# Attention and feed-forward kernel on one core: the third chunk's scores from float32 keys on 64 rows of each head

## The chip, the cores and the metric

The kernel runs on one core of one Trainium2 chip. The metric is the device time of one launch in microseconds. The kernel before was run three times: 664.55, 667.24 and 668.45 us, so its median is 667.24 us.

## The reference

A sliding-window attention with sinks, followed by a two-layer feed-forward network. Four batches, eight heads, 768 positions, 64 features per head; each query sees the first 4 positions of its batch and the last 128 positions up to itself.

```python
scores = scale * np.matmul(q, k.transpose(0, 1, 3, 2))
keep = is_sink | in_window            # pos < n_sink, or 0 <= rel < window
scores = np.where(keep, scores, -1000000000.0)
a = np.exp(scores - max); a = a / (sum + 1e-09)
x = (a @ v) as [3072, 512]            # heads side by side
h = x @ w_in                          # 512 -> 2048
g = np.where(h > 0.0, h, np.exp(np.minimum(h, 0.0)) - 1.0)
out = g @ w_out                       # 2048 -> 512
```

## The kernel before, in words

The 3072 tokens are 24 tiles of 128, cut into nine chunks of 2, 2, 2, 3, 3, 3, 3, 3 and 3 tiles. Counted from 0, the third chunk is chunk 2; it holds the last two tiles of batch 0. For each chunk there is an attention part and a feed-forward part. The attention part goes through four pairs of heads; for each pair it loads the keys and queries, makes the scores of every tile (a query tile against one or two key tiles of 132 columns, 128 keys and 4 sinks), takes the row minimum and adds the mask on VectorE (L579), the exponential on ScalarE (L581), scales and splits the probabilities into two float16 parts (L593 and L594), transposes them by a DMA (L612, `pt<-pq`), and multiplies them with the split values (L623, L628) into `po`, from which `x` is made (L636, L637). The feed-forward part makes 16 slices `h` (L664), the nonlinearity (L672 to L678, of which L678 on GpSimd makes the low part `gl`), and adds `acc` (L685).

The weights come as float64 words. During the first 150 us every one of 32 pieces is loaded (L407, `raw`) and decoded: L276 and L277 on VectorE or L271 and L272 on GpSimd, L280 on ScalarE, L282 on VectorE, then split by L429 on ScalarE and L430 on GpSimd. The first two chunks' feed-forward is done in two halves, interleaved, so that the second half of the weights is needed later.

Scores are made in two ways, chosen by the chunk's number. With `c >= DUP` and `c >= WHOLE` each head has its keys and queries twice, on rows 0 to 63 and on rows 64 to 127 (the host lays them out so). ScalarE rounds all of it to fp32r (L496), GpSimd makes the low part of the keys (L500) and, on rows 64 to 127, of the queries (L502), and TensorE makes two fp32r matmuls per head and tile on 128 rows (L553, L554). With `c < WHOLE` the two heads of a pair lie side by side on 64 rows each, and TensorE reads them as float32 from where the DMA put them (L560), one matmul per head and tile, which the trace shows as two records each:

```python
if c < WHOLE:                                                   # L486
    ld = add("SP", 0.4, lambda: nc.sync.dma_start(st[:, :kw], kq[:, o : o + kw]), ...)
    return st, None, ld, ld, users
th = add("ACT", act_us(kw), lambda: nc.scalar.activation(hi, raw, AF.Copy), deps=[ld])   # L496
```

The loads go through two buffers, `kqs0` and `kqs1`, in turn. A head's load with `c >= DUP` may overwrite its buffer once L496 and L502 have read it (L506). With `c < WHOLE` there is one load for the pair, and the buffer is free once the scores of all the chunk's tiles of that pair are made on TensorE (L574, L575). The fp32r keys go through three buffers, `kq0` to `kq2`, which are free once the scores read them (L507).

The order on every engine is written out by a planner (class `Plan`). TensorE's order is sorted by a position: slice `f` of a chunk's feed-forward has a fixed place, the scores and the value products are spread between them. The other engines and the DMA queue of SyncE (SP) are ordered by a model with costs and due times; each instruction is then chained to the one before it on its engine, so each engine and the SP queue run strictly in that order, and an instruction that waits holds up all that stand behind it.

## Time and profile before

| | us |
|---|---|
| median of three runs | 667.24 |
| lowest, highest | 664.55, 668.45 |
| span of the profiled execution | 665.4 |
| TensorE busy in the span | 610.5 |
| VectorE busy | 460.1 |
| ScalarE busy | 436.2 |
| GpSimd busy | 390.2 |

The page gives the profiled execution by its span, from the first to the last instruction; it has no other time of that execution. The median of the runs is 1.84 us above this span. The profile names the engines PE (TensorE), DVE (VectorE), ACT (ScalarE), POOL (GpSimd) and SP (the DMA queue of SyncE). In the timelines a row begins with the start and the length in us; at its end, in square brackets, stands how long the engine had been idle before it, and what released it. Rows of equal instructions that follow each other are one row, with their number behind an x.

### The profile page before, as it was taken

Reading aid. Unit: us, or ns where it says so; the run is one execution under the profiler, and the core shown is the slowest. Engines: PE = TensorE matmul, PEld = TensorE weight load, DVE = VectorE, ACT = ScalarE, POOL = GpSimd, SP = SyncE. Lnnn points to the kernel's source line nnn. Section 1 sums busy time; section 2 is a strip of 40 time slices with the busy share of each in tenths; the row PEclk is TensorE's granted clock in tenths of the full one; section 3 lists DMA queues with packets and bytes.
Section 4 is the critical chain, followed back from the end, with each engine's and each line's share of the span. In section 5 each row is a group of like instructions: output and inputs, shape, how many; then the busy total and the mean of one; then the engine's idle time right before and its main releaser. Section 6 shows DMA issues by size and latency. Waiting matters only on the chain.

```text
span 665.4 us, 13447 instructions
## 1 busy us (share of the span) xinstructions
PE 610.5 (92%) x4449; PEld 369.7 (56%) x4449; DVE 460.1 (69%) x1235; ACT 436.2 (66%) x1212; POOL 390.2 (59%) x641
## 2 busy tenths in 40 slices
PE   3477589899999999999999999999999999999995
PEld 2244356556666655555555556565555565555552
DVE  6888799997778765657677767767777776624222
ACT  4888677787778877666667776666667766523221
POOL 3599987887557766555556665554556674322221
PEclk9999689899999999999999999999999999999998
DMA  7889975746645474445444565546456723311001
GB/s 251 201 286 250 224 241 183 251 128 177 148 123 151 120 171 122 104 106 170 115 142 119 149 149 154 98 105 188 107 157 128 208 72 94 70 51 49 1 0 54
DMA packets 130110, 93.41 MB, mean 140 GB/s; under 512 B 104432, under 2 KB 109552, under 8 KB 130032
## 3 DMA queue, kind: packets, MB, share of 16 engines
q1 hardware_dynamic: 130032, 92.47, 52.2%
q8 instruction: 37, 0.61, 0.4%
q14 instruction: 41, 0.34, 0.2%
HBM read 59.94 MB, written 7.34 MB: 101 GB/s over the span
## 4 chain that ended last, share of the span: by engine, by line
PE 68%; DVE 7%; POOL 3%; DMA 3%; ACT 2%; issue 1%; POOLq 0%; ACTq 0%
PE acc L685 30%; PE h L664 30%; PE po L623 4%; PE s L553 2%; PE s L554 2%; DMA pt<-pq 2%; DVE g L674 1%; DVE wu L277 1%; DVE pq L594 1%; POOL kq L502 1%; POOL kq L500 1%; DVE wv L282 1%; POOL gl L678 1%; DVE g L675 1%; DVE wu L276 1%
## 5 line engine op out<-in xcount | busy, mean ns | idle before, releaser
L664 PE MATMUL h<-x,w 128*128 128x384 f16 (+1 forms) x1728 | 276.9, 311 | 3.3 <-DVE g L675 2.4
L664 PEld LDWEIGHTS <-w 128*128 128x128 f16 x1728 | 165.1, 98 | 96.3 <-issue 5.5
L678 POOL TENSOR_TENSOR gl<-g,gh 128x384 f16<-128x384 f32 (+1 forms) x144 | 126.7, 880 | 153.9 <-ACT gh L677 142.0
L685 PE MATMUL acc<-w,gh 128*128 128x512 f16 x768 | 195.3, 384 | 0.0
L674 DVE TENSOR_SCALAR g<-g 128x384 f32<-128x384 f32 (+1 forms) x144 | 65.6, 456 | 118.1 <-ACT g L672 118.0
L594 DVE SCALAR_TENSOR_TENSOR pq<-e,st,pq 128x256 f16<-128x256 f32 (+1 forms) x192 | 112.6, 618 | 24.6 <-ACT pq L593 24.0
L672 ACT ACTIVATE g<-h 128x384 f32<-128x384 f32 (+1 forms) x144 | 65.0, 452 | 82.1 <-PE h L664 68.9
L677 ACT ACTIVATE gh<-g 128x384 f16<-128x384 f32 (+1 forms) x144 | 69.3, 482 | 73.2 <-DVE g L675 73.1
L685 PE MATMUL acc<-w,gl 128*128 128x512 f16 x384 | 110.2, 382 | 2.8 <-POOL gl L678 2.7
L685 PEld LDWEIGHTS <-gh 128*128 128x128 f16 x768 | 71.1, 98 | 70.3 <-issue 1.8
L581 ACT ACTIVATE e<-e,st 128x264 f32<-128x264 f32 (+1 forms) x192 | 93.3, 486 | 13.1 <-DVE st L579 11.4
L593 ACT ACTIVATE pq<-e,st 128x256 f16<-128x256 f32 (+1 forms) x192 | 83.8, 479 | 9.3 <-DVE st L586 3.8
L579 DVE CUSTOM_DVE_ANT_0 e<-s,m 128x264 f32<-128x264 f32 (+1 forms) x192 | 72.5, 402 | 18.9 <-PE s L554 15.9
L500 POOL TENSOR_TENSOR kq<-kqs,kq 128x396 fp32r<-128x396 f32 (+1 forms) x56 | 67.7, 1208 | 14.4 <-ACT kq L496 9.7
L675 DVE SCALAR_TENSOR_TENSOR g<-g,h 128x384 f32<-128x384 f32 (+1 forms) x144 | 72.4, 503 | 1.8
L685 PEld LDWEIGHTS <-gl 128*128 128x128 f16 x384 | 37.5, 99 | 50.5 <-POOL gl L678 5.5
L553 PE MATMUL s<-kq 128*128 128x264 f32 x160 | 55.8, 368 | 2.8 <-POOL kq L502 2.4
L502 POOL TENSOR_TENSOR kq<-kqs,kq 64x384 fp32r<-64x384 f32 (+1 forms) x56 | 55.8, 996 | 4.4
L496 ACT ACTIVATE kq<-kqs 128x780 fp32r<-128x780 f32 (+2 forms) x56 | 48.3, 877 | 14.6 <-PE s L554 12.9
L623 PE MATMUL po<-pt,vh 128*64 128x128 f16 x704 | 42.3, 231 | 16.8 <-DMA pt<-pq 11.1
L585 POOL TENSOR_SCALAR st<-st 128x2 f32<-128x2 f32 x96 | 20.7, 216 | 59.1 <-ACT e L581 48.7
L623 PEld LDWEIGHTS <-vh 128*64 128x64 f16 x704 | 31.0, 115 | 29.2 <-issue 21.0
(80 smaller groups left out, 665.3 us busy)
## 6 DMA issues: line engine op xcount, KB each, us to landing
raw<-in_wt_dram SPq DMA_DIRECT2D x32, 512.0 KB, 5.5
kqs<-in_kq_dram SPq DMA_DIRECT2D x24, 456.0 KB, 3.3
kqs<-in_kq_dram SPq DMA_DIRECT2D x24, 390.0 KB, 3.2
out_dram<-wv SPq DMA_DIRECT2D x24, 256.0 KB, 2.3
vs<-in_vx_dram SPq DMA_DIRECT2D x20, 256.0 KB, 2.9
vm<-in_vx_dram SPq DMA_DIRECT2D x6, 768.0 KB, 4.7
kqs<-in_kq_dram SPq DMA_DIRECT2D x12, 326.0 KB, 3.7
vs<-in_vx_dram SPq DMA_DIRECT2D x12, 320.0 KB, 3.1
```

Of the source, the lines that this page charges most:

```text
L500: nc.gpsimd.tensor_tensor(buf[:, KQ_MAX : KQ_MAX + n] if c >= DUP else buf[:, kw : 2 * kw], raw[:, :n], hi[:, :n].bitcast(F32), ALU.subtract)
L579: red = add("DVE", 0.13 + 0.00145 * wd, lambda ee=ee, me=me, sp=sps[e], m=m, wd=wd: nc.vector.tensor_tensor_reduce(ee, sp[:, :wd], m[:, :w ...
L581: ex = add("ACT", 0.48 + 0.00085 * wd, lambda ee=ee, me=me, rs=rs[:, e : e + 1]: nc.scalar.activation(ee, ee, AF.Exp, bias=me, scale=-1.0, ...
L593: a = add("ACT", act_us(nb * P, True), lambda src=src, hi=hi, re=re: nc.scalar.activation(hi, src, AF.Copy, scale=re), deps=[rr])
L594: b = add("DVE", dve_us(nb * P) + 0.1, lambda src=src, hi=hi, lo=lo, re=re: nc.vector.scalar_tensor_tensor(lo, src, re, hi, ALU.mult, ALU. ...
L623: nc.tensor.matmul(po[e * D : (e + 1) * D, oc], vv[:, vo : vo + D], pt[:, (2 * e + part) * nb + i, :], start=new, stop=last)
L664: nc.tensor.matmul(hp[:, :n], win[:, part, d, :], xx[:, :n], start=k == 0, stop=k == 3 * ND - 1)
L674: b = add("DVE", 0.1 + 0.0008 * n, lambda gf=gf: nc.vector.tensor_scalar(gf, gf, -1.0, G_SCALE, ALU.add, ALU.mult), deps=[a])
L675: b = add("DVE", dve_us(n), lambda gf=gf, hp=hp: nc.vector.scalar_tensor_tensor(gf, gf, 0.0, hp[:, :n], ALU.min, ALU.max), deps=[b])
L677: th = add("ACT", act_us(n), lambda gf=gf, gh=gh: nc.scalar.activation(gh[:, :n], gf, AF.Copy), deps=[b])
L678: tl = add("POOL", pool_us(n), lambda gl=gl, gf=gf, gh=gh: nc.gpsimd.tensor_tensor(gl[:, :n], gf, gh[:, :n], ALU.subtract), deps=[th])
L685: nc.tensor.matmul(acc[i], gg[:, i * P : (i + 1) * P], wout[:, part, :], start=f == f0 and k == 0, stop=f == f1 - 1 and k == 2)
```

## The change

The scores of chunk 2 are made in the way of chunks 0 and 1. Both bounds, `WHOLE` and `DUP`, go from 2 to 3, and the layout that the host writes follows `DUP`.

```diff
 LAG = 2
-WHOLE = 2
-DUP = 2
+WHOLE = 3
+DUP = 3
 ON_POOL = range(0, 16, 2)
```

For chunk 2 the instructions of L496, L500 and L502 (eight of each) are gone, eight key loads of 128x652 become four, and 16 pairs of L553 and L554 become 16 matmuls of L560. The planner orders all engines anew.

On TensorE the places stay and only the scores change. This is the difference at the first scores of chunk 2; `s0` and `s1` are the two banks of the scores, `w9` and `w14` weight pieces.

```order
 L685 MATMUL acc1_170<-w9_141,gl1_115 128x512
-L553 MATMUL s0_166<-kq0_83 128x264
-L554 MATMUL s0_166<-kq0_83 128x264
-L553 MATMUL s1_167<-kq1_84 128x264
-L554 MATMUL s1_167<-kq1_84 128x264
+L560 MATMUL s0_166<-kqs0_70 128x264
+L560 MATMUL s1_167<-kqs0_70 128x264
 L664 LDWEIGHTS w14_146
 L664 MATMUL h1_165<-x_117,w14_146 128x256
```

Four fp32r matmuls have become two float32 matmuls, between the same neighbours.

On POOL, in the stretch just ahead of chunk 2's first scores, this stood before (`gl` is the low part of the nonlinearity, `vh0` the values' sink rows, `w` a weight piece, `wu` decoded words, `st` the softmax sums):

```order
L678 TENSOR_TENSOR gl0_114<-g1_110,gh0_111 128x256
L430 TENSOR_TENSOR w12_144<-wv0_120,w12_144 128x512
L271 TENSOR_SCALAR wu0_124<-raw2_128 128x512
L272 TENSOR_SCALAR wu0_124<-raw2_128 128x512
L529 COPY vh0_86<-vl0_88 8x128
L585 TENSOR_SCALAR st2_96<-st2_96 128x2
L678 TENSOR_TENSOR gl1_115<-g0_109,gh1_112 128x256
L500 TENSOR_TENSOR kq0_83<-kqs0_70,kq0_83 128x396
L502 TENSOR_TENSOR kq0_83<-kqs0_70,kq0_83 64x256
L500 TENSOR_TENSOR kq1_84<-kqs1_71,kq1_84 128x396
L502 TENSOR_TENSOR kq1_84<-kqs1_71,kq1_84 64x256
L585 TENSOR_SCALAR st3_97<-st3_97 128x2
```

And this stands there now:

```order
L678 TENSOR_TENSOR gl0_114<-g1_110,gh0_111 128x256
L600 TENSOR_TENSOR st0_94<-e0_91,st0_94 128x8
L603 CAST pq0_100<-st0_94 128x2x8
L604 TENSOR_TENSOR pq0_100<-st0_94,pq0_100 128x8
L272 TENSOR_SCALAR wu0_124<-raw0_126 128x512
L600 TENSOR_TENSOR st1_95<-e1_92,st1_95 128x8
L603 CAST pq1_101<-st1_95 128x2x8
L604 TENSOR_TENSOR pq1_101<-st1_95,pq1_101 128x8
L529 COPY vh0_86<-vl0_88 8x128
L430 TENSOR_TENSOR w9_141<-wv1_121,w9_141 128x512
L430 TENSOR_TENSOR w12_144<-wv0_120,w12_144 128x512
L678 TENSOR_TENSOR gl1_115<-g0_109,gh1_112 128x256
```

`gl0` has moved ahead of two groups of sink rows, of L272 and of `w9`; `vh0` has moved ahead of `w9`, of `w12` and of a pair of L271 and L272; the four key instructions between `gl1` and `st3` are gone.

On the SP queue, around the loads of chunk 3's first heads (128x780; `kqs0` for the even heads, `kqs1` for the odd ones), this stood before. `pt2` to `pt5` belong to the fifth to eighth of chunk 2's eight steps (a step is one pair of heads at one tile), `vs` is a load of values, `wv3` a reload of a saved partial sum:

```order
L520 DMA vs0_72<-in_vx_dram 128x512
L495 DMA kqs1_71<-in_kq_dram 128x780
L612 DMA_TRANSPOSE pt2_105<-pq2_102 128x9x128
L612 DMA_TRANSPOSE pt3_106<-pq0_100 128x9x128
L705 DMA wv3_123<-out_0_dram 128x512
L520 DMA vs1_73<-in_vx_dram 128x512
L495 DMA kqs0_70<-in_kq_dram 128x780
```

And this stands there now, where the first load into `kqs1` comes:

```order
L495 DMA kqs0_70<-in_kq_dram 128x780
L520 DMA vs0_72<-in_vx_dram 128x512
L612 DMA_TRANSPOSE pt4_107<-pq1_101 128x9x128
L495 DMA kqs1_71<-in_kq_dram 128x780
L612 DMA_TRANSPOSE pt5_108<-pq2_102 128x9x128
L495 DMA kqs1_71<-in_kq_dram 128x780
L612 DMA_TRANSPOSE pt0_103<-pq0_100 128x4x128
```

The load of chunk 3's second head, the first into `kqs1`, stood ahead of `pt2` and stands now between `pt4` and `pt5`; it waits there for TensorE, because the scores of chunk 2's last pair of heads read `kqs1` themselves.

## Rows read from the trace of the kernel before

**Rows 1.** The page, its first line and part 1: busy time of each engine in us, share of the span, instructions.

```profile
span 665.4 us, 13447 instructions
...
PE 610.5 (92%) x4449; PEld 369.7 (56%) x4449; DVE 460.1 (69%) x1235; ACT 436.2 (66%) x1212; POOL 390.2 (59%) x641
```

**Rows 2.** Busy time of each engine in stretches of 20 us (us from the start, length, busy us of each engine with the number of instructions), then the granted TensorE clock, the busy share of the DMA engines and GB/s.

```profile
60.00:80.00 20.00, 11.35 (x89) 6.78 (x83) 15.63 (x33) 13.93 (x38) 18.46 (x27) 0.74 0.95 264
80.00:100.00 20.00, 16.24 (x124) 10.88 (x125) 18.55 (x39) 15.60 (x41) 17.25 (x25) 0.91 0.86 217
100.00:120.00 20.00, 17.11 (x137) 11.64 (x135) 19.32 (x38) 14.28 (x40) 14.96 (x22) 0.98 0.61 182
120.00:140.00 20.00, 18.21 (x135) 11.77 (x133) 20.00 (x44) 16.86 (x45) 16.41 (x22) 0.93 0.61 203
140.00:160.00 20.00, 18.70 (x148) 12.72 (x146) 15.98 (x40) 14.20 (x45) 16.86 (x29) 1.00 0.71 182
```

**Rows 3.** TensorE's timeline from 60 to 157 us: the rows with the longest waits.

```profile
62.82 0.30 PE L623 MATMUL po<-pt,vh 128*64 128x128 f16 x4 [2.70 <-DMA pt<-pq]
...
67.83 0.87 PE L685 MATMUL acc<-w,gl 128*128 128x512 f16 x2 [2.15 <-POOL gl L678]
...
72.50 0.32 PE L628 MATMUL po<-pt,vh 128*64 128x128 f16 x2 [3.02 <-POOL vh L529]
...
80.04 1.38 PE L664 MATMUL h<-x,w 128*128 128x256 f16 x11 [0.83 <-POOL w L430]
84.67 0.30 PE L623 MATMUL po<-pt,vh 128*64 128x128 f16 x4 [3.25 <-DMA pt<-pq]
...
118.52 2.08 PE L664 MATMUL h<-x,w 128*128 128x256 f16 x12 [1.43 <-DVE g L675]
```

**Rows 4.** POOL's timeline from 67 to 78 us, with the first four key instructions of chunk 2.

```profile
67.10 0.68 POOL L678 TENSOR_TENSOR gl<-g,gh 128x256 f16<-128x256 f32 x1
...
72.16 0.28 POOL L529 COPY vh<-vl 8x128 f16<-8x128 f16 x1
...
73.43 1.50 POOL L500 TENSOR_TENSOR kq<-kqs,kq 128x396 fp32r<-128x396 f32 x1
75.01 0.79 POOL L502 TENSOR_TENSOR kq<-kqs,kq 64x256 fp32r<-64x256 f32 x1
75.88 1.08 POOL L500 TENSOR_TENSOR kq<-kqs,kq 128x396 fp32r<-128x396 f32 x1
77.03 0.72 POOL L502 TENSOR_TENSOR kq<-kqs,kq 64x256 fp32r<-64x256 f32 x1
```

**Rows 5.** The timelines of VectorE and of POOL from 93 to 98 us: one VectorE operation without and with a key instruction beside it, and the key instructions.

```profile
93.33 0.45 DVE L277 TENSOR_SCALAR wu<-raw 128x512 uint16<-128x512 uint16 x1
...
96.86 1.29 DVE L277 TENSOR_SCALAR wu<-raw 128x512 uint16<-128x512 uint16 x1
...
96.75 1.08 POOL L500 TENSOR_TENSOR kq<-kqs,kq 128x396 fp32r<-128x396 f32 x1
97.91 0.80 POOL L502 TENSOR_TENSOR kq<-kqs,kq 64x256 fp32r<-64x256 f32 x1
```

**Rows 6.** TensorE's timeline: a pair of heads by float32 matmuls in chunk 1, back to back and behind a wait, and a pair by fp32r matmuls in chunk 2, each with the row that follows it.

```profile
50.29 0.72 PE L560 MATMUL s<-kqs 64*128 64x264 f32 x4
50.93 1.48 PE L664 MATMUL h<-x,w 128*128 128x256 f16 x12
...
54.59 1.06 PE L560 MATMUL s<-kqs 64*128 64x264 f32 x4 [0.88 <-DVE st L579]
55.59 0.30 PE L623 MATMUL po<-pt,vh 128*64 128x128 f16 x4
...
102.18 0.48 PE L553 MATMUL s<-kq 128*128 128x264 f32 x1
...
102.86 1.48 PE L664 MATMUL h<-x,w 128*128 128x256 f16 x12
```

**Rows 7.** The start of chunk 3: TensorE's last scores of chunk 2 and what follows, then ScalarE's and POOL's work on the keys of chunk 3's second head, then TensorE's scores of that head.

```profile
156.51 0.48 PE L553 MATMUL s<-kq 128*128 128x264 f32 x1
...
157.19 1.49 PE L664 MATMUL h<-x,w 128*128 128x256 f16 x12
...
157.27 0.84 ACT L496 ACTIVATE kq<-kqs 128x780 fp32r<-128x780 f32 x1
...
158.19 1.02 POOL L500 TENSOR_TENSOR kq<-kqs,kq 128x396 fp32r<-128x396 f32 x1
159.29 1.14 POOL L502 TENSOR_TENSOR kq<-kqs,kq 64x384 fp32r<-64x384 f32 x1
...
160.48 0.33 PE L553 MATMUL s<-kq 128*128 128x132 f32 x1 [0.35 <-POOL kq L502]
```

**Rows 8.** Key loads: two loads of chunk 1 on the SP queue in one row (the first stands at its start), the scores that waited for the first of them, and, from the view of L495, the time from issue to landing of its 56 loads.

```profile
38.85 5.31 SPq L489 DMA_DIRECT2D kqs<-in_kq_dram  x2
...
44.73 0.90 PE L560 MATMUL s<-kqs 64*128 64x264 f32 x4 [0.93 <-DMA kqs<-in_kq_dram]
...
DMA to landing us min/median/max: 3.0/3.3/6.3
```

**Rows 9.** TensorE's timeline from 165 to 240 us: two waits that remain.

```profile
183.04 0.30 PE L623 MATMUL po<-pt,vh 128*64 128x128 f16 x4 [0.97 <-DMA pt<-pq]
...
216.45 0.39 PE L553 MATMUL s<-kq 128*128 128x264 f32 x1 [1.22 <-POOL kq L502]
```

## The prediction

> **What bounds the kernel now.** I read the page's first part, then the busy times by stretches of 20 us, then TensorE's timeline where these show holes, and last the timelines of the engines that ended its waits. TensorE is busy 610.5 of 665.4 us [rows 1], so little but its own idle time and its clock can be gained. From 60 to 160 us it is busy for 81.61 of 100 us (the sum of the five stretches, 11.35 to 18.70), at a granted clock down to 0.74 [rows 2]. In these 100 us POOL is busy for 83.94 and VectorE for 89.48; VectorE has no pause at all from 120 to 140 us, and the DMA engines are at 0.95 from 60 to 80 us [rows 2]. So this stage, where the weights are decoded beside the attention of chunks 1 to 3, is bounded by POOL first and by VectorE later, and TensorE waits for them. Its long waits are of that kind: 2.15 us for `gl`, 3.02 for `vh`, 0.83 for a weight piece (all three made by POOL), 2.70 and 3.25 for transposed probabilities, 1.43 for VectorE [rows 3]. From 160 us on TensorE is nearly always at work, and only an added wait there would count.
>
> **The change, part by part.** All is summed against the span of the profiled execution, 665.4 us; the median of the runs is 667.24, so 1.84 us more, and I carry the difference over to the median.
>
> *TensorE's scores.* A pair by fp32r takes from 102.18 to 102.86, 0.68 us; a pair by float32 takes from 50.29 to 50.93, 0.64 us, back to back behind other matmuls, and 1.00 us (54.59 to 55.59) behind a wait [rows 6]. Chunk 2 has eight such pairs and most stand between busy neighbours: 8 x -0.04 = -0.3 us. Bounds: -0.3 to 8 x 0.32 = +2.6.
>
> *A rule that speaks against the change* is in the Trainium skill, "FP8 and Floating Point Precision", section "TensorE Precision Notes": a true float32 matmul goes through the array in four passes. As an estimate by that page, two heads of four passes of 264 columns at 2.4 GHz are 0.88 us a pair, and the term would be 8 x 0.20 = +1.6 us in place of -0.3. The row with 0.64 us is below that, so I keep the row.
>
> *Less work on POOL, ScalarE and the DMA queue.* Eight L500 and eight L502 go; the four that the rows show take 1.50, 0.79, 1.08 and 0.72, together 4.09 us from 73.43 on [rows 4], so the eight heads are some 15 to 16 us of POOL (1.88 for the head at 96.75 [rows 5]), of the 83.94 that it works in this stage. Eight ScalarE copies and four of eight loads go as well.
>
> What of this reaches TensorE: the wait of 0.83 for a weight piece and that of 3.25 for transposes come behind the four key instructions, whose 4.09 us stand ahead of `st3` and what follows it; both go, -4.1. The waits for `gl` (2.15) and `vh` (3.02) come ahead of them, but the planner has moved both instructions forward on POOL, `gl0` past an L272, the piece `w9` and six short ones, `vh0` past `w9`, `w12` and a pair of L271 and L272; what it moved back is still owed, so I count half of 5.17, -2.6. The clock of 0.74 and 0.91 in the first two stretches stands for some 10.4 and 3.6 us at 1.2 in place of 2.4 GHz (twice the missing share of 20 us); less the 3.02 us of waiting among them, half of the rest, 5.5 us, is what this costs, and with less idle time I count a quarter of it, -1.4. Sum: -8.1 by the end of chunk 2.
>
> Is VectorE able to follow? From 80 to 140 us it is busy for 57.87 of 60 us [rows 2], so TensorE can keep a lead only if VectorE gets through earlier as well. The rows say that it does: L277 takes 0.45 us alone and 1.29 beside a key instruction [rows 5], 0.84 us given back per L500. If a head costs it one such delay and a fourth more for its L502, eight heads give back 8 x 1.05 = 8.4 us. That covers the lead, but barely. Bounds of the whole gain: below nothing, +2.7 us, if the planner's new order of the early loads, with the DMA engines at 0.95, repeats the wait of 2.70 at one more place; at most the four waits (9.25) and all the lost clock (5.5), -14.8. I take -8.1.
>
> *A new wait at the start of chunk 3.* Before, the keys of chunk 3's second head were loaded long ahead; what ended last was the fp32r buffer, free after chunk 2's last scores: ScalarE copies at 157.27, POOL makes the low parts from 158.19 to 160.43, TensorE goes on at 160.48, 0.35 us late [rows 7]. Now `kqs1` is read by chunk 2's last scores themselves, so the load can only be issued after these, and the same copy and low parts come after the load. What is added to the path is the load: 3.3 us (3.0 to 6.3) and some 0.15 for the queue, +3.45. Between them TensorE has the same work as before, one `h`, one `acc` and the first head's scores, so nothing hides it. Behind the waiting load on SP stand `pt5`, the load of the fourth head and `pt0`; `pt5` needs the same scores and its values are due much later, so they cost nothing more. A load that waited in the same manner in chunk 1 was issued at 38.85 and its scores came at 44.73 [rows 8], 5.9 us, with the DMA engines busier. Bounds: 3.1 to 6.5.
>
> TensorE would then idle for 0.35 + 3.45 = 3.8 us. After the waits of 3.02 and 3.25 it ran at 1.2 GHz for a while (clock 0.74 and 0.91 in these stretches [rows 2, 3]); I add 1.5 us for that, between 0 and 2. Once TensorE is late by this, a wait such as the 0.97 us at 183.04 shrinks, while the 1.22 at 216.45 hangs on TensorE's own scores and stays [rows 9]: -0.5.
>
> Sum: -0.3 - 8.1 + 3.45 + 1.5 - 0.5 = -3.95 us. From 667.24 that is 663.3.
>
> **The rivals.**
>
> *The gain is larger.* All four waits on POOL go (-9.25) with half of the lost clock (-2.7), and the new wait costs its smallest value, 3.1, without a fall of the clock: -0.3 - 11.95 + 3.1 = -9.15 us, 658.1. For it: POOL is the busiest engine from 60 to 80 us. Against it: VectorE's 57.87 of 60 us afterwards, which can give back 8.4 at best by the rows.
>
> *Given back.* VectorE stays the bound up to 140 us, and its delays beside key instructions turn into delays beside L430 and `gl`, which move up into the free places. Then the lead at chunk 2's end is what VectorE saves, perhaps half of 8.4, 4.2 us, and the new wait takes it: -0.3 - 4.2 + 4.45 = 0, 667.2. A price of float32 pairs of 1.00 us, as behind a wait, ends here too: -3.95 + 2.9 = -1.05, 666.2. The four passes of the Trainium skill's page would put it at -3.95 + 1.9 = -2.05, 665.2, by that estimate.
>
> *Slower.* The load at chunk 3's start costs what the one at 38.85 cost, 5.9 us in place of 3.3, since `pt4`, itself late if TensorE runs ahead of the engines that make it, stands before it on SP: 5.9 + 0.15 + 2 for the clock = +8.05, and the lead is only 3, since the waits for `gl` and `vh` reappear as waits for the weight pieces that were moved back: 667.24 - 0.3 + 8.05 - 3 = 672.0. It decides as soon as the new wait with its clock is over 3.3 us more than the lead. For it: the load has nothing to hide behind. Against it: from 140 to 160 us the DMA engines are at 0.71 only.
>
> That the change doesn't do what it says can be left out: the order shows all eight pairs as float32.
>
> **How the numbers follow.** Half a per cent, 3.3 us, is about what a measurement of this kernel can tell from no change. Chances: the sum above, taken as faster by over 3.3 us, 0.34; the larger gain 0.13; given back, within 3.3 us on either side, 0.34; slower 0.19. That makes faster 0.47, same 0.34, slower 0.19. (Of the 0.34, 0.05 stand for dearer float32 pairs, by the row of 1.00 us.) The rule of the Trainium skill's page would come out in that same part. The predicted time is that of the sum, 663.3, whose own range is 660 to 664. The range for 8 in 10 reaches from 656, below the larger gain's 658.1 but short of the bound of -14.8, to 670.5, short of the slower case's 672.0.
>
> **What would show it right or wrong.** Right: chunk 2's last scores come some 8 us earlier than 156.51; the waits for `vh` and for the weight piece between 60 and 90 us are gone; VectorE's L277 in this stage has fewer long instances; TensorE waits some 3.8 us at the first scores of chunk 3's second head, with the load of these keys, ScalarE's copy and POOL's low part before it; from there to the end the distance is that of before plus what the clock loses. Wrong: chunk 2's last scores come less than 5 us earlier (then the lead was mis-sized), the wait at chunk 3's start is below 3 or above 6 us, a pair of float32 scores takes 0.9 us or more between busy neighbours, or new waits of over a microsecond show up before 60 us or behind 170 us.

## The result and the profile after the change

| | median us | runs | lowest, highest |
|---|---|---|---|
| before, beside it | 668.45 | 9 | 664.55, 670.07 |
| after | 672.04 | 9 | 671.16, 673.95 |

The ratio over the runs is 1.0077 with a 95% interval of 1.0052 to 1.0101: the changed kernel is slower by 0.8%. (The two medians alone are 0.5% apart, since the times of before scatter over 5.5 us.) The forecast was 663.3, and the whole range to 670.5 lies below the result. The profiled execution of after took 673.17 us, of which 671.4 are its span; it lies 1.1 us above the median of after. Its span is 6.0 us above that of before, while the medians differ by 3.6, so distances read between these two traces are larger than those between the medians.

The page's first line and part 1 of after, against [rows 1]:

```profile
span 671.4 us, 13386 instructions
...
PE 615.1 (92%) x4449; PEld 368.6 (55%) x4449; DVE 454.0 (68%) x1235; ACT 432.0 (64%) x1204; POOL 375.5 (56%) x625
```

POOL has lost 14.7 us of work, a little under the forecast 15 to 16, ScalarE 4.2 and VectorE 6.1; none of them sets the end. Then the busy times in stretches of after, against [rows 2] (columns as there); the last row is a part of the one above it:

```profile
60.00:80.00 20.00, 14.68 (x149) 9.10 (x147) 17.09 (x41) 15.26 (x41) 18.04 (x27) 0.91 0.83 238
80.00:100.00 20.00, 16.47 (x116) 10.51 (x117) 17.18 (x39) 14.51 (x39) 12.13 (x21) 0.83 0.72 200
100.00:120.00 20.00, 19.86 (x153) 12.57 (x152) 19.09 (x42) 15.12 (x44) 14.09 (x22) 1.00 0.69 202
120.00:140.00 20.00, 16.05 (x127) 9.79 (x126) 19.44 (x43) 15.60 (x43) 13.53 (x17) 1.00 0.51 166
140.00:160.00 20.00, 18.75 (x145) 11.84 (x145) 15.40 (x42) 13.77 (x41) 15.96 (x30) 1.00 0.78 205
160.00:180.00 20.00, 15.82 (x114) 10.66 (x114) 8.18 (x30) 11.28 (x35) 6.91 (x10) 0.83 0.31 71
163.70:169.00 5.30, 5.25 (x20) 3.06 (x21) 1.70 (x7) 1.91 (x7) 0.86 (x2) 0.50 0.24 75
```

From 100 to 120 us TensorE works 2.75 us more than before, at a full clock: here is a gain. From 120 to 140 us it works 2.16 us less, although POOL has only 13.53 us to do, and VectorE is still busy for 19.44 of 20. From 160 to 180 us, where the same view of before has TensorE busy for 19.23 us, it has 15.82 here, and VectorE, GpSimd and the DMA engines have little to do either (8.18, 6.91 and a share of 0.31): one chain is being waited for. TensorE's timeline of after says which, against [rows 3, 6, 7] (idle time and releaser in brackets):

```profile
69.53 0.30 PE L623 MATMUL po<-pt,vh 128*64 128x128 f16 x4 [1.26 <-DMA pt<-pq]
73.85 0.42 PE L623 MATMUL po<-pt,vh 128*64 128x128 f16 x4 [3.55 <-DMA pt<-pq]
80.45 1.37 PE L664 MATMUL h<-x,w 128*128 128x256 f16 x11 [0.95 <-POOL w L430]
84.23 0.42 PE L623 MATMUL po<-pt,vh 128*64 128x128 f16 x4 [2.40 <-DVE wu L276]
...
136.07 1.47 PE L664 MATMUL h<-x,w 128*128 128x256 f16 x12 [2.61 <-DVE g L675]
139.91 1.38 PE L664 MATMUL h<-x,w 128*128 128x256 f16 x11 [0.95 <-POOL w L430]
...
155.47 0.72 PE L560 MATMUL s<-kqs 64*128 64x264 f32 x4
156.12 1.48 PE L664 MATMUL h<-x,w 128*128 128x256 f16 x12
...
163.75 0.48 PE L553 MATMUL s<-kq 128*128 128x132 f32 x1 [4.69 <-POOL kq L502]
164.25 2.78 PE L664 MATMUL h<-x,w 128*128 128x256 f16 x12
```

Three things are to be seen. The waits between 60 and 90 us have changed their names and have not gone: `gl` and `vh` no longer hold TensorE, but the transposes do, and the weight piece at 80 us still does. Chunk 2's last scores come at 155.47, 1.04 us earlier than the 156.51 of [rows 7], not 8. And the forecast wait at chunk 3's second head is there, 4.69 us in place of 0.35, and behind it twelve `h` matmuls take 2.78 us in place of 1.48: after an idle time of 4.69 us the granted clock was at its lower level, 1.2 GHz (0.50 of full speed), from 163.7 to 169 us.

The timelines of SP, ScalarE and POOL of after for the same wait (before: [rows 7]):

```profile
155.51 1.39 SPq L612 DMA_TRANSPOSE pt<-pq  x1
156.96 1.14 SPq L495 DMA_DIRECT2D kqs<-in_kq_dram  x1
...
160.68 0.85 ACT L496 ACTIVATE kq<-kqs 128x780 fp32r<-128x780 f32 x1 [1.46 <-DMA kqs<-in_kq_dram]
...
161.61 1.02 POOL L500 TENSOR_TENSOR kq<-kqs,kq 128x396 fp32r<-128x396 f32 x1 [2.51 <-ACT kq L496]
162.71 0.99 POOL L502 TENSOR_TENSOR kq<-kqs,kq 64x384 fp32r<-64x384 f32 x1
```

The chain is load, copy, low part, scores, one behind the other, with nothing between. The scores that free `kqs1` end at 156.12, but the load is issued at 156.96, when `pt4` has left the queue (155.51 and 1.39 us). From there it takes 3.72 us to the start of the copy, and the copy and the low parts take 3.07 us to the scores at 163.75.

To see where time was won and lost, TensorE's landmarks serve better than its waits: the start of the first L664 matmul of each slice `h`, counted over all parts of the feed-forward from 0. Slices 7 to 28 run beside the attention of chunk 2: slice 7 follows its first scores and slice 28 its last. Each number is that start in one kernel minus that in before, from the two traces (the five right columns are told of below). The profiled executions of e1, e6 and after lie -0.5, +0.1 and +1.1 us from their medians, those of e5, e7 and e12 +0.9, +1.0 and -1.4.

| slice | start before | after | e1 | e5 | e6 | e7 | e12 |
|---|---|---|---|---|---|---|---|
| 0 | 36.07 | +3.0 | +0.1 | +0.2 | +0.3 | +0.3 | +2.6 |
| 14 | 107.14 | +1.3 | -0.7 | +2.1 | +1.3 | +0.2 | -0.6 |
| 18 | 122.80 | -3.1 | -4.0 | +2.1 | -2.0 | -3.1 | -4.6 |
| 21 | 133.82 | -3.8 | -3.4 | +2.1 | -1.3 | -2.5 | -5.3 |
| 22 | 137.60 | -1.5 | -3.8 | +2.4 | -1.7 | -2.9 | -3.0 |
| 28 | 157.19 | -1.1 | -4.4 | +2.4 | -2.3 | -3.9 | -2.5 |
| 30 | 163.38 | +5.9 | -4.8 | +2.0 | -2.7 | +1.3 | -2.3 |
| 56 | 263.79 | +6.2 | -4.3 | +1.8 | -2.9 | +1.8 | -1.3 |

In after, TensorE begins 3.0 us late at slice 0, ahead of all of chunk 2's scores; this comes with the new order (e12, which has it too, is 2.6 late there, and the runs with the order of before at most 0.3). By slice 8 all but 0.4 us of it is made up, as TensorE comes later and waits less between 60 and 90 us (waits of 0.4 us and more sum to 8.84 us there, in before to 12.41). Then 3.8 us are won by slice 21, 2.3 of them are lost again between slices 21 and 22, and 6.9 between slices 28 and 30 (4.6 of waiting, 2.4 of clock). From there to the end the distance stays.

### The profile page after: what moved, and what is told of

It reads as the page before. It is cut to its first block, busy times and chain, and to the rows that moved or that the text cites. A ratio compares the mean times of both kernels' runs of the same rounds, so it can differ in the third digit from the quotient of the medians.

```text
span 671.4 us, 13386 instructions
## 1 busy us (share of the span) xinstructions
PE 615.1 (92%) x4449; PEld 368.6 (55%) x4449; DVE 454.0 (68%) x1235; ACT 432.0 (64%) x1204; POOL 375.5 (56%) x625
## 4 chain that ended last, share of the span: by engine, by line
PE 68%; POOL 3%; DMA 3%; DVE 2%; ACT 2%; issue 2%; POOLq 0%; ACTq 0%
PE acc L685 30%; PE h L664 30%; PE po L623 3%; PE s L553 2%; DMA pt<-pq 2%; PE s L554 2%; POOL kq L500 1%; POOL kq L502 1%; DMA kqs<-in_kq_dram 1%; ACT kq L496 1%; POOL gl L678 1%; PE po L628 0%; DVE g L674 0%; ACT pq L593 0%; DVE e L579 0%
## 5 line engine op out<-in xcount | busy, mean ns | idle before, releaser
L664 PE MATMUL h<-x,w 128*128 128x384 f16 (+1 forms) x1728 | 279.7, 313 | 4.5 <-DVE g L675 2.6
L664 PEld LDWEIGHTS <-w 128*128 128x128 f16 x1728 | 166.4, 99 | 101.0 <-issue 7.3
L674 DVE TENSOR_SCALAR g<-g 128x384 f32<-128x384 f32 (+1 forms) x144 | 63.6, 441 | 119.3 <-ACT g L672 118.6
L500 POOL TENSOR_TENSOR kq<-kqs,kq 128x396 fp32r<-128x396 f32 (+1 forms) x48 | 58.1, 1210 | 20.4 <-ACT kq L496 15.0
L553 PE MATMUL s<-kq 128*128 128x264 f32 (+1 forms) x144 | 49.9, 366 | 6.5 <-POOL kq L502 6.3
L496 ACT ACTIVATE kq<-kqs 128x780 fp32r<-128x780 f32 (+1 forms) x48 | 42.5, 902 | 17.3 <-PE s L554 14.1
L502 POOL TENSOR_TENSOR kq<-kqs,kq 64x384 fp32r<-64x384 f32 x48 | 48.9, 1018 | 3.8
```

Of the source, the lines that this page charges most:

```text
L500: nc.gpsimd.tensor_tensor(buf[:, KQ_MAX : KQ_MAX + n] if c >= DUP else buf[:, kw : 2 * kw], raw[:, :n], hi[:, :n].bitcast(F32), ALU.subtract)
L664: nc.tensor.matmul(hp[:, :n], win[:, part, d, :], xx[:, :n], start=k == 0, stop=k == 3 * ND - 1)
```

## The experiments

Each was run beside the kernel before on the same chip, and the ratio is to those runs of it; e1 to e4 were on one chip, e5 to e8 on a second, e9 to e12 on a third. Differences between runs of different chips are therefore best read from the ratios. In the edits ` ...` stands for lines left out.

| run | median us | ratio, 95% interval |
|---|---|---|
| e1_before_order | 664.10 | 0.9952 [0.9932, 0.9973] |
| e2_after_own | 674.55 | 1.0102 [1.0079, 1.0126] |
| e3_after_early | 670.42 | 1.0044 [1.0030, 1.0059] |
| e4_after_three_buffers | 664.53 | 0.9949 [0.9928, 0.9970] |
| e5_scores_only | 668.65 | 1.0019 [0.9997, 1.0041] |
| e6_no_low_parts | 664.24 | 0.9957 [0.9938, 0.9975] |
| e7_late_load | 668.51 | 1.0022 [0.9999, 1.0045] |
| e8_after_moves | 674.30 | 1.0116 [1.0086, 1.0146] |
| e9_early_low_behind | 672.59 | 1.0079 [1.0048, 1.0109] |
| e10_only_load_early | 673.02 | 1.0082 [1.0056, 1.0109] |
| e11_before_three_buffers | 674.36 | 1.0112 [1.0081, 1.0142] |
| e12_after_spread | 667.08 | 0.9997 [0.9974, 1.0020] |

My theory after the result: the relief of POOL is worth little, since VectorE's decode holds the stage, and the new wait with its clock, 6.9 us, makes the kernel slower. The rival: the relief is worth the 8 us of the forecast, and the planner's new order gives it away.

### The gain without the new order

**e1_before_order.** The planner plans the work of before, so that every engine keeps its order; what chunk 2 no longer needs is left empty, and its scores read float32 pairs from four buffers of their own.

```diff
+PLANNED = 2
 ...
+    own = rows("own", [P, len(key_tiles(CHUNKS[2])) * KW + len(CHUNKS[2]) * P], F32, NP)
 ...
-            buf = kqr[slot("kq")] if c >= WHOLE else None
+            buf = kqr[slot("kq")] if c >= PLANNED else None
 ...
+            if c == 2:
+                pair = own[h // 2][:, :kw]
+                load = (lambda: None) if h % 2 else lambda: nc.sync.dma_start(pair, kq[:, o : o + kw])
+                ld = add("SP", 0.4, load, lat=dma_us(P * kw * 4))
+                th = add("ACT", act_us(kw), lambda: None, deps=[ld])
+                tl = add("POOL", pool_us(kc) + pool_us(qc), lambda: None, deps=[th])
 ...
```

> The order of every engine is that of the kernel before; chunk 2's scores are float32 matmuls from four buffers of their own, and its copies, low parts and second loads are left out of the queues. Theory A (VectorE and the weight decode hold this stage, so relief of POOL is worth little): chunk 2's last scores come 0 to 2 us earlier than the 156.51 of before, the time is 0 to 2 us below before. Theory B (the relief is worth the forecast 8 us, and the planner's new order of the first 60 us ate it): chunk 2's last scores come 6 to 9 us earlier, the time is 5 to 9 us below before.

Measured: 3.4 us faster than before, between the two theories; chunk 2's last scores come at 152.16, 4.35 us earlier than in before. The change of the scores is a gain where no other instruction changes its place, so the loss is in the order or in the shared buffers, which e2 below takes apart.

**e5_scores_only and e6_no_low_parts** split this gain. From here on theory A says that the relief of the other engines brings these 3.4 us, and that the new order and the wait lose more. In e5 the loads, copies and low parts of chunk 2 all stay, read by nobody; in e6 only the low parts go: the body of `low` is empty there. The edit is that of e5 against e1.

```diff
-                load = (lambda: None) if h % 2 else lambda: nc.sync.dma_start(pair, kq[:, o : o + kw])
-                th = add("ACT", act_us(kw), lambda: None, deps=[ld])
 ...
+                src = st[:, :kw] if h % 2 else pair
+                th = add("ACT", act_us(kw), lambda: nc.scalar.activation(hi, src, AF.Copy), deps=[ld])
+                def low():
+                    nc.gpsimd.tensor_tensor(buf[:, KQ_MAX : KQ_MAX + kc], src[:, :kc], hi[:, :kc].bitcast(F32), ALU.subtract)
+                    nc.gpsimd.tensor_tensor(hi[D:, kc:], src[D:, kc:], hi[D:, kc:].bitcast(F32), ALU.subtract)
 ...
```

> The order of before on every engine. Only the scores of chunk 2 change: float32 pairs from four buffers of their own; all eight loads, eight ScalarE copies and sixteen POOL low parts of chunk 2 stay, though nothing reads them. Theory A (the relief of the other engines brings the 3.4 us of e1_before_order, the float32 scores themselves next to nothing): 8 x -0.04 = -0.3 us on TensorE, and since the scores no longer wait for a low part up to -1 more; ratio to before 0.998 to 1.0. Rival B (what helps is that the scores wait for a DMA only, not for the chain copy, low part, scores; the relief brings nothing): 664 to 665 us, ratio 0.994 to 0.997. Rival C (the float32 pairs are dearer, 1.00 us as behind a wait, and the relief hides it in e1_before_order): 8 x 0.32 = +2.6 us, ratio 1.004.

> As e5_scores_only, with the sixteen low parts of chunk 2 (L500, L502) left out as well; loads and copies stay. Theory A with POOL as the stage's bound: nearly all of the 3.4 us of e1_before_order is POOL's, 664 to 665 us, ratio 0.995 to 0.997. Rival (ScalarE's copies and the DMA loads bring as much as POOL): about half, 665.8 us, ratio 0.9975. Rival (POOL brings nothing, since VectorE holds the stage either way): as e5_scores_only.

Measured: e5 no faster than before (its interval holds 1), e6 664.24, as fast as e1. The interval of e5 also reaches rival C's 1.004, but that rival's price of a pair is not there: between busy neighbours the pairs of e5 take 0.65 us (104.70 to 105.35). So the float32 scores themselves bring nothing that can be told from zero, neither do ScalarE's copies and the four loads, and POOL's sixteen low parts are the whole gain, 668.65 - 664.24 = 4.4 us.

This is a difference of medians. Of the 29 executions of before that ran beside e5 and e6, from 663.82 to 670.37 us, nine lie under 665.5 us, where all twelve of e6 lie (and one of e5, 664.94). So some executions reach this time with the low parts in place. None of them is among the traces, and what they do differently stays open.

How the gain comes to TensorE is seen in the two timelines, which hold the same instructions in the same order but for the low parts (L495 and L496 here). First e5, of VectorE, POOL and TensorE, and a row of its busy times in stretches:

```profile
109.27 1.29 DVE L278 TENSOR_SCALAR wu<-raw 128x512 uint16<-128x512 uint16 x1
...
121.84 1.27 DVE L277 TENSOR_SCALAR wu<-raw 128x512 uint16<-128x512 uint16 x1
...
109.19 1.04 POOL L495 TENSOR_TENSOR kq<-own,kq 128x396 fp32r<-128x396 f32 x1
...
121.77 1.02 POOL L495 TENSOR_TENSOR kq<-kqs,kq 128x396 fp32r<-128x396 f32 x1
...
72.99 0.25 PE L645 MATMUL po<-pt,vh 128*64 128x128 f16 x2 [3.57 <-POOL vh L546]
80.52 2.52 PE L681 MATMUL h<-x,w 128*128 128x256 f16 x11 [1.65 <-POOL w L432]
85.12 0.42 PE L640 MATMUL po<-pt,vh 128*64 128x128 f16 x4 [2.08 <-DMA pt<-pq]
...
120.67 1.93 PE L681 MATMUL h<-x,w 128*128 128x256 f16 x12 [1.43 <-DVE g L692]
...
122.70:125.00 2.30, 2.30 (x7) 0.81 (x6) 2.30 (x7) 1.69 (x6) 1.99 (x5) 0.51 1.05 385
```

The same in e6, which has no wait for a weight piece at 80 us:

```profile
108.13 0.45 DVE L278 TENSOR_SCALAR wu<-raw 128x512 uint16<-128x512 uint16 x1
...
119.41 0.44 DVE L277 TENSOR_SCALAR wu<-raw 128x512 uint16<-128x512 uint16 x1
...
73.09 0.32 PE L644 MATMUL po<-pt,vh 128*64 128x128 f16 x2 [2.95 <-POOL vh L545]
85.67 0.42 PE L639 MATMUL po<-pt,vh 128*64 128x128 f16 x4 [4.45 <-DMA pt<-pq]
...
118.23 1.47 PE L680 MATMUL h<-x,w 128*128 128x256 f16 x12 [1.03 <-DVE g L691]
...
120.50:123.00 2.50, 2.38 (x17) 1.47 (x15) 2.09 (x5) 2.50 (x8) 2.03 (x3) 1.00 1.04 407
```

In these rows a decode instruction that starts just behind a low part ends only after it: 109.19 + 1.04 = 110.23, and the L278 beside it ends at 110.56. The Trainium skill, "SBUF — State Buffer", section "Who interferes with whom", says that VectorE's `tensor_scalar` in a two-port mode and a GpSimd instruction shut each other out for the whole length of whichever came first; the trace agrees in the times, with 1.29 and 0.45 us, but does not show whether L278 runs in such a mode. Without the low part VectorE has the nonlinearity `g` done earlier, TensorE waits 1.03 in place of 1.43, and its clock does not fall behind that wait (granted 0.51 from 122.7 to 125 us in e5, 1.00 from 120.5 to 123 in e6). Between slices 14 and 18 e6 wins 3.3 us on e5, and 1.7 of them are this clock: from slice 17 to 18, with no wait between, e5 takes 4.27 us and e6 2.60. The relief of POOL works for the most part through VectorE, and not through the waits between 60 and 90 us: these sum to 11.32 us in e5 and to 12.25 in e6. The wait for the weight piece goes (1.65 to none), but that for the transposes at 85 us grows from 2.08 to 4.45, and `vh` holds TensorE in both (3.57 and 2.95; 3.56 in e1).

### The wait at the start of chunk 3

**e2_after_own** takes the order of after and gives chunk 2's pairs buffers of their own, so that the load for chunk 3's second head waits for no scores; its place on SP stays.

```diff
+            if c == 2:
+                st = own[h // 2]
```

> The changed kernel with its own order, but chunk 2's pairs lie in four buffers of their own, so the load of chunk 3's second head no longer waits for scores; its place on the SP queue stays. Theory A (the place on the queues makes the wait, behind pt4 on SP): the wait at chunk 3's second head stays above 4 us and the time is within 1 us of the changed kernel. Theory B (the buffer's wait alone makes it): the wait falls below 1 us and the time is 5 to 7 us below the changed kernel.

Measured: no gain, and the wait is there as in after, from TensorE's timeline of e2:

```profile
163.60 0.48 PE L556 MATMUL s<-kq 128*128 128x132 f32 x1 [4.55 <-POOL kq L505]
```

With the buffer free, the load is still issued behind `pt4` (at 156.75; 156.96 in after), so its place is enough to make the wait. This also clears the shared buffers of the loss that e1 left open.

**e7_late_load** is the converse: e1 with this one DMA issue moved behind `pt4`. In the edits from here on, `marks` holds the instructions to be moved; the lines that fill it are left out.

```diff
+    tasks.remove(marks["load"])
+    tasks.insert(tasks.index(marks["pt4"]) + 1, marks["load"])
```

> As e1_before_order, with one DMA issue moved: the load of chunk 3's second head stands behind pt4 on the SP queue, where the changed kernel has it, instead of ahead of pt2; its buffer is free long before. ScalarE's copy and POOL's low parts keep their places. Theory A (the place behind pt4 costs the time at chunk 3's start, since nothing is between pt4 and the scores): pt4's issue at about 150.7, the load 1.5 us later, 3.3 us to land, copy 0.9, low parts 2.1, so the scores at about 158.5 in place of 155.7: a wait of 3 to 4 us and up to 2 us of clock behind it, 667 to 670 us against 664.1 for e1_before_order, that is +3 to +6. Rival B (place of the load alone matters little; in the changed kernel the copy and the low part also stand later on ScalarE and POOL, and these make the wait): under +1.5 us, 664 to 665.6.

Measured: 668.51 (668.21 without one execution of 2199.88 us, which the ratio leaves out), 0.7% above e1 by the ratios, and the whole gain is gone. The timeline of e7, of SP, ScalarE, POOL and TensorE:

```profile
151.47 2.12 SPq L626 DMA_TRANSPOSE pt<-pq  x1
153.64 6.76 SPq L507 DMA_DIRECT2D kqs<-in_kq_dram  x2
...
157.02 0.85 ACT L508 ACTIVATE kq<-kqs 128x780 fp32r<-128x780 f32 x1 [3.77 <-DMA kqs<-in_kq_dram]
...
159.05 0.99 POOL L514 TENSOR_TENSOR kq<-kqs,kq 64x384 fp32r<-64x384 f32 x1
...
160.10 0.37 PE L567 MATMUL s<-kq 128*128 128x132 f32 x1 [3.83 <-POOL kq L514]
```

**e10_only_load_early** moves in the order of after (with e2's buffers) that load alone, ahead of `pt2` (`marks["before"]`).

```diff
+    tasks.remove(marks["load"])
+    tasks.insert(tasks.index(marks["before"]), marks["load"])
```

> As e2_after_own, with the load of chunk 3's second head ahead of pt2 on SP; ScalarE's copy and POOL's low parts stay at their late places. Theory A (the place of the load is most of the wait): ScalarE's copy starts right behind the two probabilities at 159.2 in place of 160.68, so the scores come 1.4 us earlier; with the late places of copy and low part the rest of the wait, some 3 us, stays: 672.5 to 673.5 us against 674.55 for e2_after_own, ratio 1.007 to 1.009. Rival B (the load alone is the wait, as e7_late_load's +4.4 us may suggest): nearly all of 4.5 us and of the clock behind it goes, 668 to 669.5 us, ratio 1.001 to 1.003.

Measured: 673.02, as theory A has it. TensorE still waits, in its timeline of e10:

```profile
163.49 0.48 PE L560 MATMUL s<-kq 128*128 128x132 f32 x1 [3.17 <-POOL kq L509]
```

So the late place of the load alone gives a wait of 3.83 us, and the late places of copy and low parts together give 3.17 without it. The copy's and the low parts' places were not tried singly.

**e3_after_early, e8_after_moves, e9_early_low_behind** move copy and low parts forward as well, straight behind those of the first head (`w31` is the last weight piece; e9: the low parts behind `w31`; e8: both heads' low parts behind `w31`, and on VectorE the nonlinearity of slice 20 ahead of the decode pair). `marks[0]` and `marks[1]` are load, copy and low parts of the first and of the second head; the diff is that of e3.

```diff
+    for t, at in zip(marks[1], (marks["before"], marks[0][1], marks[0][2])):
+        tasks.remove(t)
+        tasks.insert(tasks.index(at) + (at is not marks["before"]), t)
```

> As the one above, and the load, the copy and the low part of chunk 3's second head are also moved forward on their three queues: the load ahead of pt2, the copy and the low part behind those of the first head. Theory A (the late load costs its wait of 4.7 us and 2.2 us of slower clock behind it, 6.9 in all, and little else differs): the wait is gone, the clock stays at 2.4 GHz at 164 us, the time is 6 to 7 us below the changed kernel, 0 to 2 below before. Theory B (TensorE's delay is made up or taken over by the next wait, so it costs half): 3 us below the changed kernel.

> The order of the changed kernel with e3_after_early's early load, copy and two further moves: the low parts of chunk 3's first two heads stand behind POOL's last weight piece (w31) instead of ahead of it, and the two VectorE instructions of the nonlinearity of slice 20 (counted over all parts) stand ahead of the decode pair L276, L277 at 132.15 and 133.47, not behind it. Theory A (the changed kernel lost its lead in three places: 2.6 us waiting for g at 136.07, 4.7 and 2.2 at chunk 3's start): the wait for g shrinks to under 0.7, the wait for w31 that e3_after_early had at 149.74 (1.56) goes, and the lead of 3.8 to 4.9 us that stood at slice 21 lasts to the end: 663 to 665.5 us, ratio 0.994 to 0.997. Rival B (the lead at slice 21 is only borrowed: VectorE has the same decode work left, and the wait for g comes back at the next pair of slices): 668 to 670 us, ratio 1.001 to 1.004.

> As e3_after_early, with one thing put elsewhere: the low parts of chunk 3's second head stand on POOL behind the last weight piece (w31) instead of ahead of it. Nothing else moves. Theory A (e3_after_early lost its 2.6 us between slices 24 and 26 to these 2.0 us of POOL ahead of w31; without that the changed order has no wait left at chunk 3's start and keeps the distance of slice 24): slice 28 comes 1 to 2 us before that of the kernel before, 665.5 to 667 us, ratio 0.997 to 0.9995, so the changed order is hardly faster than before even without its wait. Rival B (the wait at 149.74 had another cause, or comes back as a wait for gl or for the low part): as e3_after_early, 669 to 671 us, ratio 1.002 to 1.005. Rival C (all of the gain of e1_before_order is in the changed order too): 664 us, ratio 0.995.

Measured: 670.42, 674.30 and 672.59. The wait of 4.7 us is gone in all three, but each carries a wait that the edit itself made. e3 lies 1.6 us below after by the medians and misses both of its theories, 6 to 7 and 3. The copy now stands so early that ScalarE waits for its load (1.90 us in e3, 2.35 in e8, 2.01 in e9), and `w31` stands behind it; from ScalarE's timeline of e9:

```profile
147.82 0.86 ACT L501 ACTIVATE kq<-kqs 128x780 fp32r<-128x780 f32 x1 [2.01 <-DMA kqs<-in_kq_dram]
```

So e8 and e9, which I made to mend e3, left this in place, and theory A fell in both. They added a second wait: the low parts behind `w31` now stand ahead of the `gl` that TensorE needs next, and it waits for that 5.06 us in e8 and 2.85 in e9. From e8's timelines of TensorE and ScalarE one thing can still be read, since it lies ahead of this copy:

```profile
133.00 0.27 PE L673 MATMUL h<-x,w 128*128 128x256 f16 x1 [0.46 <-DVE g L684]
133.56 1.38 PE L673 MATMUL h<-x,w 128*128 128x256 f16 x11 [0.29 <-POOL w L431]
...
136.06 1.04 PE L695 MATMUL acc<-w,gh 128*128 128x512 f16 x4 [1.13 <-ACT gh L687]
...
137.90 0.28 PE L673 MATMUL h<-x,w 128*128 128x256 f16 x1 [0.36 <-ACT w L430]
...
135.03 0.65 ACT L280 ACTIVATE acc<-raw 128x512 f32<-128x512 f32 x1 [1.50 <-DVE wv L282]
```

With `g` first, the wait of 2.6 us for it shrinks to 0.46, but 1.13 for the nonlinearity's next step, `gh`, and 0.29 and 0.36 for weight pieces follow, and at slice 23 the distance to before is -2.3, that of e3 -2.6. The decode itself is late there: ScalarE waits 1.50 us for VectorE's decoded words, and `gh` stands behind that. So the 2.3 us that after loses between slices 21 and 22 had been borrowed from VectorE's decode, as far as this one move shows. In after's timeline of VectorE and POOL the pair ahead of `g` stands beside two instructions L430, which lengthen it as the low parts did:

```profile
132.15 1.42 DVE L276 TENSOR_SCALAR wu<-raw 128x512 uint16<-128x512 uint16 x1
133.47 1.39 DVE L277 TENSOR_SCALAR wu<-raw 128x512 uint16<-128x512 uint16 x1
134.76 0.29 DVE L674 TENSOR_SCALAR g<-g 128x256 f32<-128x256 f32 x1
...
135.60 0.41 DVE L675 SCALAR_TENSOR_TENSOR g<-g,h 128x256 f32<-128x256 f32 x1
...
132.09 2.45 POOL L430 TENSOR_TENSOR w<-wv,w 128x512 f16<-128x512 f32 x2 [1.74 <-ACT w L429]
```

**e12_after_spread** puts the three steps where their engines have a gap: the load ahead of `pt2`, the copy four ScalarE tasks behind `w31`'s, the low parts ten POOL tasks behind `w31`'s.

```diff
+    ld, th, tl = marks[1]
 ...
+    tasks.insert(tasks.index(marks["before"]), ld)
+    for t, behind, n in ((th, w_done[31][0], 4), (tl, w_done[31][1], 10)):
+        at = [u for u in tasks[tasks.index(behind) + 1 :] if u.eng == t.eng][n - 1]
+        tasks.insert(tasks.index(at) + 1, t)
```

> The order of the changed kernel with e2_after_own's buffers, and the three steps of chunk 3's second head put where their engines have a gap: the load ahead of pt2 on SP; ScalarE's copy behind the second e after w31's first half, where ScalarE idles 1.5 us in e2_after_own; POOL's low parts behind the third gl after w31, just ahead of st5. In e3_after_early and e9_early_low_behind the copy stood right behind the first head's and made ScalarE wait 2.0 us for the load, with w31 behind it, so these two runs carried a wait of their own. Theory A (the wait of 4.7 us and the clock behind it are all that chunk 3's start costs; what the changed order has gained until there is only the 1.0 us of slice 28, against 4.4 in e1_before_order): no wait over 0.5 us from 145 to 165 us, slice 28 still 0.5 to 1.5 us ahead of before, 666 to 668 us, ratio 0.998 to 1.001: no slower than before, but 2 to 4 us behind e1_before_order. Rival B (with the wait gone, a new one shows up at chunk 3's start, as in the runs before): 669.5 us or more, ratio 1.003 or more. Rival C (the whole gain was hidden by the wait): 664 us, ratio 0.995.

Measured: 667.08, ratio 0.9997: no slower than before, 0.8% less than after and 0.5% more than e1 by the ratios. TensorE's timeline of e12:

```profile
134.59 1.47 PE L673 MATMUL h<-x,w 128*128 128x256 f16 x12 [2.62 <-DVE g L684]
...
158.19 0.33 PE L560 MATMUL s<-kq 128*128 128x132 f32 x1 [0.50 <-POOL kq L507]
```

Theory A holds in the time: the wait at chunk 3's start and the clock behind it are what makes after slower than before. Its landmark came out further ahead than expected, 2.5 us at slice 28 in place of 0.5 to 1.5, in a trace that lies 1.4 us below its median; the longest wait from 145 to 165 us is 0.55 us, for a transpose. The loss for `g` (still there) and some of slices 22 to 56 are what remains against e1 in the traces.

### A third buffer

**e4_after_three_buffers** and **e11_before_three_buffers** change one number, in after and in before; the planner orders all engines anew in both.

```diff
-RINGS = dict(kqs=2, kq=3, vs=2, vm=1, vhl=2, e=3, st=6, pq=3, pt=6, g=2, gh=3, x=7, wv=4, s=2, po=1, h=2, wu=2, sv=2, wps=1, raw=6)
+RINGS = dict(kqs=3, kq=3, vs=2, vm=1, vhl=2, e=3, st=6, pq=3, pt=6, g=2, gh=3, x=7, wv=4, s=2, po=1, h=2, wu=2, sv=2, wps=1, raw=6)
```

> The changed kernel with three buffers for key loads in place of two, ordered anew by the planner, so that no load of chunk 3 waits for chunk 2's last scores. Theory A: no wait above 1 us at chunk 3's start, the time 4 to 8 us below the changed kernel, the spread being what a new order does. Theory B (the wait is the planner's choice whatever the buffers): a wait above 3 us stays, the time within 2 us of the changed kernel.

> The kernel before, its scores untouched, with a third buffer for loaded keys, so that the planner orders all engines anew. It tells whether e4_after_three_buffers is faster by the change of the scores or by the buffer and another order. Theory A (the relief of POOL by the float32 scores is what helps; the low parts are still made here): 665.5 to 669.5 us, ratio 0.997 to 1.003. Rival B (the third buffer, or a luckier order, helps by itself): 664.5 us or less, ratio 0.995.

Measured: 664.53 and 674.36. With a third buffer the planner puts the load ahead of `pt4` by itself (issued at 146.18), no wait stands at chunk 3's start, and the time is that of e1. The same buffer without the change of the scores makes the kernel slower by 1.1%, so the buffer does not help by itself. But both kernels have a new order, and e11 shows how far that alone can move the time: 7 us with the same work. So how much of e4's gain is the scores and how much a luckier order is not shown. Why the order of e11 is worse was not followed up. e1, e6 and e4 beat both kernels.

## Why the prediction was wrong, point by point

The terms of after's trace, from the table: -1.1 us at slice 28, +4.6 for the wait, +2.4 for the clock and +0.3 from slice 30 to 56, together +6.2 (the two traces differ by 6.0, the medians by 3.6). The forecast had -8.4, +3.45, +1.5 and -0.5.

**The scores, -0.3: right, as far as it can be told.** A pair takes from 155.47 to 156.12, 0.65 us, and e5 lies 1.0 us above before, with an interval from -0.2 to +2.7 us. The four passes of the Trainium skill, "FP8 and Floating Point Precision", section "TensorE Precision Notes", which an estimate made 0.88 us a pair, don't show as such a time in this trace. The estimate added the passes of both heads, while the trace has the four records of a pair start two and two (155.47, 155.47, 155.79 and 155.80), so the two heads run side by side and the 0.65 us does not speak against four passes for each.

**The relief, -8.1: the term that failed.** At chunk 2's last scores 1.0 us was left of it. The step said that the waits for the weight piece and for the transposes, 4.1 us, go with the four key instructions ahead of them. They don't: 0.95 and 2.40 us stand there in after, and in e1, with no other place changed, three waits of 1.0 to 1.4 us; in e6, where only the low parts go, one of 4.45. Of the waits for `gl` and `vh` I counted half; both names are gone in after, and two waits for transposes of 1.26 and 3.55 took their place. I summed waits of an early stretch, where TensorE is held by several engines in turn, as if each wait were removed with the work ahead of it. What the relief is worth by the runs is 4.4 us (e5 to e6), and most of it comes later, from 107 to 123 us, by way of VectorE and of the clock behind its wait. That way was in the text, as the cover of 8.4 us that VectorE gets back; it was not the cover but the gain, at half its size. And the new order spent most of it ahead of chunk 3: 2.3 us between slices 21 and 22.

**The new wait, +3.45 and 0.35: right in kind, too small.** 4.69 us. The sum had the load issued as soon as the scores free the buffer, and called what stands on SP behind the load harmless; it left what stands ahead of it to a rival. The issue came 0.84 us later for that, and the load took 3.72 us to the start of the copy. e2 shows that the buffer doesn't matter: the load, the copy and the low parts all have late places, and the load's alone, or those of the other two, make most of the wait (e7, e10).

**The clock, +1.5:** 2.4 us between slices 29 and 30, above the bound of 2. **The later waits, -0.5:** the distance rather grows by 0.3 from slice 30 to 56.

**The rivals.** The slower one came, and its condition with it: the wait with its clock exceeds the lead by over 3.3 us (6.9 against 1.1). It named `pt4` as what stands before the load. That its 672.0 is nearly the median is partly luck: its load of 5.9 us did not come (3.72), and it set the wait with its clock to 8.05 and the lead to 3. "Given back" was right that L430 delays VectorE's decode in place of the key instructions, as the rows at 132 us show. I gave the slower case 0.19, because I took the large lead for likely; by e1 and e6, a lead of 3.4 to 4.4 us is what the removed work can bring, and against a wait of 3.8 us and 1.5 of clock that alone would have made "same" or "slower" the likeliest.

## What to carry to other kernels

A change that takes work off one engine and is planned anew is two changes; run the work's removal with the order frozen, and the order's change with the work kept, before reading either from the sum. Where a buffer is read longer than before, follow every step that refills it, on each queue: an early load is worth little (0.2% from e2 to e10) while the copy and the low parts behind it keep late places, and a copy that comes too early holds up its own engine. And a wait that follows a removed instruction need not go with it; in a stretch where several engines are busy, the next one takes over.

## What the runs showed that I had not expected

In this kernel POOL's low parts cost more through VectorE's decode than through POOL's own queue: one low part of 1.04 us lengthened an instruction of 0.45 to 1.29, and taking sixteen of them away was worth 4.4 us of the median though TensorE's wait for `vh`, which POOL makes, hardly changed (3.57 us in e5, 2.95 in e6). And the same three steps, a load, a copy and two low parts, at five sets of places gave 674.55 (e2), 673.02 (e10), 672.59 (e9), 670.42 (e3) and 667.08 (e12), with the same work on every engine.
